# A fused MLP kernel on one core: the transpose of tile 2 moved ahead of weight slab 2 on SyncE's queue

## The chip, the core and the metric

The kernel runs on one core of a Trainium2 chip. The metric is the device time of one execution in microseconds (us), as the median over runs. Beside the timed runs one execution is profiled; its trace has the start and duration of every instruction on each engine, the semaphore events, and the DMA packets. In the profile's rows PE is TensorE's matmul, PEld its weight load, DVE VectorE, ACT ScalarE, POOL GpSimd and SP SyncE. A "q" behind an engine (SPq) marks what its sequencer does, here the issue of a DMA.

## What is computed

A two-layer perceptron with SiLU between the layers, in bfloat16, with x of 2048 x 640, w1 of 640 x 1728 and w2 of 1728 x 640:

```python
def reference(x, w1, w2):
    h = jnp.einsum("bsd,df->bsf", x, w1)
    h = _silu(h)
    out = jnp.einsum("bsf,fd->bsd", h, w2)
    return out
```

## The kernel before

**Layout.** The first layer is computed transposed: `hT` holds h with its 1728 features on partitions (13 tiles of 128 and one of 64) and the 2048 tokens along the free side. A matmul takes 64 columns of `w1s` as weights and streams 512 tokens of `xT`; `step` (line 179) issues the two halves of one feature tile, and the five `k` tiles of the depth 640 accumulate in PSUM. `xT` is x transposed: [128, 5 tiles of depth, 2048 tokens]. x comes from memory through DMA transposes straight into `xT`, w1 through plain loads into `w1s`.

**The opening.** The tokens go in four chunks of 512. For chunk 0 the data have not all arrived when TensorE could begin, so the loop is turned inside out: eight feature tiles (`NO` = 8) hold the eight PSUM banks, and `sweep` runs once for each depth tile k over all eight. Sweep k needs tile k of `xT` and *slab* k of w1 (rows of depth tile k, columns 0 to 1023, 256 KB). Slab 0 comes in two parts: columns 0 to 639 on ScalarE's queue (slab 0a, 160 KB) and 640 to 1023 on SyncE's (slab 0b, 96 KB). Before the first data TensorE runs matmuls on a tile of zeros (`first_dummies`). `opening` then runs sweeps 0, 1 and 2; the lines behind it run 3 and 4. After sweep 4 of a feature tile ScalarE applies SiLU and writes `hT`. Then come feature tiles 8 to 12 of chunk 0, with the remaining columns of w1 (`ld_rest`, `ld_rest2`), and chunks 1 to 3, whose transposes are 15 further DMAs (line 159).

**The queue.** Nearly all DMAs are issued by SyncE, which takes its instructions in order. `early` puts an instruction into the program's first block, ahead of that engine's part in the barrier that closes the block; several calls for SyncE stand there in the order in which they were made. The order of the opening on SyncE is: transpose of tiles 0 and 1; slab 0b; slab 1; slab 2; transpose of tile 2; slab 3; transpose of tiles 3 and 4; slab 4; then, behind the barrier, the rest of w1, the 15 transposes, and w2. `turned` (line 90) issues a transpose, `load` (line 85), called by `slab`, a plain load. Each has a semaphore of its own.

**Who waits.** TensorE alone waits for these transfers. Sweep 0 waits for the transpose of tiles 0 and 1 and slab 0a, and at feature tile 5 (`NA`) for slab 0b; sweeps 1 and 2 wait for their slab and their tile, through

```python
            for k in (1, 2):
                sweep(k, 0, SCH, ld_w1[k], ld_t[k])
```

where `ld_t[1]` is the same event as `ld_t[0]`; sweep 3 waits for slab 3 and the transpose of tiles 3 and 4, sweep 4 for slab 4.

**The second layer** begins when all of h is there. It runs in quads of output tiles whose two halves of the contraction share the array, evicts PSUM by VectorE and ScalarE in turn and stores the output. None of it touches the lines of the change.

Of the kernel before, what the change touches and what calls it, by code (L numbers as in the profile page):

```python
# [9 lines left out]
def bass_standalone__dense_activation_silu__prompt_kernel(  # L10
# [16 lines left out]
    DT = D // P  # L27
    FT = F // P
    FL = F - FT * P
    SCH = 512  # L30
# [10 lines left out]
    with ExitStack() as es:  # L41
# [18 lines left out]
        def sem(name):  # L60
            s = es.enter_context(nc.semaphore(name))
            count[s.name if hasattr(s, "name") else name] = 0
            return [s, 0]

        def tick(ins, s, n=1):
            ins.then_inc(s[0], n)
            s[1] += n
            return (s, s[1])
# [16 lines left out]
        def load(eng, out_ap, in_ap):  # L85
            s = sem(f"s_ld{n_dma[0]}")
            n_dma[0] += 1
            return tick(eng.dma_start(out=out_ap, in_=in_ap), s, 16)

        def turned(c0, c1, k0, k1):  # L90
            s = sem(f"s_tr{n_dma[0]}")
            n_dma[0] += 1
            return tick(sp.dma_start_transpose(
                out=xT[:, k0:k1, c0:c1], in_=xf[c0:c1, k0 * P:k1 * P]), s, 16)

        ET = mybir.EngineType

        def early(emit, engine, arrived=True):
            n = len(nc.main_func.blocks[0].instructions)
            r = emit()  # L100
            lst = nc.main_func.blocks[0].instructions
            new = lst[n:]
            del lst[n:]
            at = next(
                i for i, ins in enumerate(lst)
                if ins.opcode == ("EventSemaphore" if arrived else "Drain") and ins.engine == engine
            )
            lst[at:at] = new
            return r
# [8 lines left out]
        def slab(eng, k, f0=0, f1=NO):  # L118
            return load(eng, w1s[:, k, f0 * P:f1 * P], w1_v[:, k, f0 * P:f1 * P])

        ld_w1 = {}
        ld_t = {}
# [18 lines left out]

        ld_w1b = early(lambda: slab(sp, 0, NA, NO), ET.SP, False)
        ld_w1[1] = early(lambda: slab(sp, 1), ET.SP, False)
        ld_w1[2] = early(lambda: slab(sp, 2), ET.SP, False)
        ld_t[2] = early(lambda: turned(0, SCH, 2, 3), ET.SP, False)
        ld_w1[3] = early(lambda: slab(sp, 3), ET.SP, False)
        ld_t[3] = ld_t[4] = early(lambda: turned(0, SCH, 3, DT), ET.SP, False)
        ld_w1[4] = early(lambda: slab(sp, 4), ET.SP, False)
        CM = CO + 2 * P
        ld_rest = load(sp, w1s[:, :, CO:CM], w1_v[:, :, CO:CM])  # L150
# [259 lines left out]
```

## Time and profile before

| | |
|---|---|
| Median of 3 runs | 124.75 us (124.65 to 124.89) |
| The profiled execution's own time | 124.91 us |
| Its span, first to last instruction | 123.4 us |
| TensorE matmul busy | 121.1 us |
| TensorE weight load busy | 59.5 us |
| ScalarE busy | 38.8 us |
| VectorE busy | 7.0 us |
| DMA, whole span | 10.42 MB |
| Granted TensorE clock, mean | 1.000 |

Times in the trace count from the span's start, so they are 1.5 us short of the device time as a whole (124.91 - 123.4), which lies around the span. In a row of the timeline the first number is the start, the second the length from the first instruction's start to the last one's end, and "x" the count. The square brackets give the idle time of the engine ahead of the row and what ended it. In the list of DMA issues the last number is the time from the issue to the last of the transfer's semaphore increments. A matmul's recorded end is a model, so a TensorE that reads as busy may still have waited inside; the starts of its weight loads are recorded.

### The profile page before, as it was taken

What the parts mean: (1) busy time and instruction counts of PE and PEld (TensorE: products, weight loads), DVE (VectorE), ACT (ScalarE), POOL (GpSimd) and SP (SyncE); (2) the same over time, 40 slices, a digit from 0 to 9 for tenths busy, and PEclk for the clock granted to TensorE, in tenths of its full rate; (3) what the DMA queues carried; (4) which work ended last, traced back from release to release, by engine and by line L of the source; (5) the groups of instructions that cost most, each with busy time, mean ns of one, the idle gap of its engine ahead of it and who ended that gap; (6) DMA issues with size and microseconds to landing.
All of it is one profiled execution on the core that took longest, in us unless ns stands there. A gap on an engine that the chain in (4) does not pass through costs nothing.

```text
span 123.4 us, 2299 instructions
## 1 busy us (share of the span) xinstructions
PE 121.1 (98%) x1057; PEld 59.5 (48%) x1057; DVE 7.0 (6%) x11; ACT 38.8 (31%) x67; POOL 0.3 (0%) x5
## 2 busy tenths in 40 slices
PE   8999999999999999999999999999999999999993
PEld 5455555555555555555544444444444444444452
DVE  0000000000000000000000022002201300222001
ACT  0041985555555555555530011001101200110110
POOL 0000000000000000000000000000000000000000
PEclk9999999999999999999999999999999999999999
DMA  6999945475992000000000005202200220022112
GB/s 142 234 271 302 157 103 108 94 75 92 288 391 70 0 0 0 8 0 0 0 0 5 0 5 115 56 0 106 106 0 5 106 106 0 5 106 106 53 74 86
DMA packets 19482, 10.42 MB, mean 84 GB/s; under 512 B 13457, under 2 KB 18961, under 8 KB 19473
## 3 DMA queue, kind: packets, MB, share of 16 engines
q1 hardware_dynamic: 19184, 10.05, 32.1%
q10 hardware_dynamic: 288, 0.23, 0.8%
q8 instruction: 8, 0.13, 0.5%
q14 instruction: 2, 0.01, 0.0%
HBM read 4.51 MB, written 2.62 MB: 58 GB/s over the span
## 4 chain that ended last, share of the span: by engine, by line
PE 95%; DMA 3%; ACT 0%; issue 0%
PE ps L171 95%; DMA xT<-in_x_dram 3%; ACT o_sb L254 0%
## 5 line engine op out<-in xcount | busy, mean ns | idle before, releaser
L171 PE MATMUL ps<-xT,w1s 128*64 128x512 bf16 x540 | 59.2, 382 | 0.1
L171 PE MATMUL ps<-w2s,hT 64*128 64x512 bf16 (+3 forms) x377 | 46.2, 369 | 0.0
L171 PEld LDWEIGHTS ps<-xT,w1s 128*64 128x64 bf16 x540 | 30.5, 111 | 28.6 <-issue 0.9
L175 ACT ACTIVATE hT<-ps 128x512 bf16<-128x512 f32 x52 | 30.0, 607 | 22.9 <-PE ps L171 22.9
L171 PEld LDWEIGHTS ps<-w2s,hT 64*128 64x128 bf16 (+1 forms) x377 | 21.0, 95 | 24.1 <-issue 0.2
L254 ACT CAST o_sb<-ps 128x512 bf16<-128x512 f32 (+1 forms) x9 | 5.0, 551 | 41.5 <-PE ps L171 41.5
L171 PE MATMUL ps<-hT,w2s 64*128 64x512 bf16 x104 | 11.7, 376 | 0.0
L171 PEld LDWEIGHTS ps<-hT,w2s 64*128 64x128 bf16 x104 | 5.0, 94 | 6.3 <-issue 0.4
L252 DVE CAST o_sb<-ps 128x512 bf16<-128x512 f32 (+1 forms) x8 | 5.4, 675 | 40.5 <-PE ps L171 40.5
L252 DVE CAST oT<-ps 128x512 bf16<-128x512 f32 x2 | 1.4, 692 | 73.8 <-PE ps L171 73.8
L254 ACT CAST oT<-ps 128x512 bf16<-128x512 f32 x2 | 1.2, 586 | 10.6 <-PE ps L171 10.6
L132 PE MATMUL ps<-z 128*128 128x256 bf16 (+1 forms) x15 | 3.3, 419 | 0.4 <-DVE z L125 0.4
L153 ACT ACT_TABLE_LOAD x1 | 1.3, 1283 | 7.1 <-DVEq L395 7.1
L171 PE MATMUL ps<-w2t,hTt 64*128 64x512 bf16 (+2 forms) x17 | 2.9, 363 | 0.0
L132 PEld LDWEIGHTS ps<-z 128*128 128x128 bf16 (+1 forms) x15 | 1.9, 142 | 1.5 <-issue 0.4
L175 ACT ACTIVATE hTt<-ps 128x512 bf16<-128x512 f32 x2 | 1.2, 597 | 1.0 <-PE ps L171 1.0
L171 PEld LDWEIGHTS ps<-w2t,hTt 64*128 64x128 bf16 x17 | 0.9, 94 | 1.1
L171 PE MATMUL ps<-hTt,w2t 64*128 64x512 bf16 x4 | 0.8, 376 | 0.0
L171 PEld LDWEIGHTS ps<-hTt,w2t 64*128 64x128 bf16 x4 | 0.2, 94 | 0.2
L153 ACT ACTIVATE warm<-warm 128x32 f32<-128x32 f32 x1 | 0.2, 229 | 0.0
L125 DVE MEMSET z<- 128x128 uint32 x1 | 0.2, 165 | 0.2 <-issue 0.2
L140 POOL MEMSET warm<- 128x32 f32 x1 | 0.1, 125 | 6.7 <-POOLq L395 6.7
(4 smaller groups left out, 0.4 us busy)
## 6 DMA issues: line engine op xcount, KB each, us to landing
out_dram<-o_sb SPq DMA_DIRECT2D x15, 160.0 KB, 1.8
w2s<-in_w_dram SPq DMA_DIRECT2D x1, 1120.0 KB, 6.1
w1s<-in_w_dram SPq DMA_DIRECT2D x4, 256.0 KB, 3.9
w2s<-in_w_dram SPq DMA_DIRECT2D x1, 960.0 KB, 8.4
w1s<-in_w_dram SPq DMA_DIRECT2D x1, 560.0 KB, 5.5
w1s<-in_w_dram SPq DMA_DIRECT2D x1, 320.0 KB, 4.3
xT<-in_x_dram SPq DMA_TRANSPOSE x18, 3.9
w1s<-in_w_dram ACTq DMA_DIRECT2D x1, 160.0 KB, 2.7
```

The source lines that it names most:

```text
L125: p_z = early(lambda: tick(dve.memset(z[:, :], 0.0), s_dve), ET.DVE, False)
L132: pe.matmul(ps[c0:c0 + w, 3, 0:HB], lhsT=z[:, 0:w], rhs=z[:, :], start=True, stop=True)
L140: p_warm = tick(pool.memset(warm[:, :], 0.0), s_pool)
L153: act.activation(out=warm[:, :], in_=warm[:, :], func=ACT.Silu)
L171: return pe.matmul(o, lhsT=l, rhs=r, start=start, stop=stop, skip_group_check=shared)
L175: r = tick(act.activation(out=out_ap, in_=in_ap, func=ACT.Silu), s_act)
L252: r = tick(dve.tensor_copy(out=out_ap, in_=in_ap), s_dve)
L254: r = tick(act.copy(out=out_ap, in_=in_ap), s_act)
```

## The change

The transpose of tile 2 is made one place earlier on SyncE's queue, ahead of slab 2 instead of behind it. Slabs 2 and 3 then stand next to each other. In the transpose of tiles 3 and 4 the upper bound `DT` is written as 5, which is its value.

```diff
         ld_w1b = early(lambda: slab(sp, 0, NA, NO), ET.SP, False)
         ld_w1[1] = early(lambda: slab(sp, 1), ET.SP, False)
+        ld_t[2] = early(lambda: turned(0, SCH, 2, 3), ET.SP, False)
         ld_w1[2] = early(lambda: slab(sp, 2), ET.SP, False)
-        ld_t[2] = early(lambda: turned(0, SCH, 2, 3), ET.SP, False)
         ld_w1[3] = early(lambda: slab(sp, 3), ET.SP, False)
-        ld_t[3] = ld_t[4] = early(lambda: turned(0, SCH, 3, DT), ET.SP, False)
+        ld_t[3] = ld_t[4] = early(lambda: turned(0, SCH, 3, 5), ET.SP, False)
         ld_w1[4] = early(lambda: slab(sp, 4), ET.SP, False)
```

The order on SyncE is then: transpose of tiles 0 and 1; slab 0b; slab 1; transpose of tile 2; slab 2; slab 3; transpose of tiles 3 and 4; slab 4. The waits of the sweeps are written as before.

## The prediction

> **What bounds the kernel now.** I read the page first: its span line, its busy rows and its chain of work that ended last.
>
> ```profile
> span 123.4 us, 2299 instructions
> PE 121.1 (98%) x1057; PEld 59.5 (48%) x1057; DVE 7.0 (6%) x11; ACT 38.8 (31%) x67; POOL 0.3 (0%) x5
> PE 95%; DMA 3%; ACT 0%; issue 0%
> ```
>
> The chain in order of time then says where those 3% of DMA lie.
>
> ```profile
> 0.00 3.72 DMA xT<-in_x_dram
> 3.72 0.04 issue
> 3.76 117.77 PE ps L171 x1041
> ```
>
> There is one DMA on the path: the first transpose (tiles 0 and 1), which lands at 3.72. From 3.76 to 121.53 TensorE runs matmul after matmul and the chain never leaves it. So the reordered transfers matter only if one of them now lands too late, or if the first transpose moves. A busy PE row does not prove that nothing waits, because matmul ends are modelled; so I went to the weight loads (PEld) in the timeline of the first 30 us, whose starts are not.
>
> ```profile
> 3.76 0.18 PEld L171 LDWEIGHTS ps<-xT,w1s 128*64 128x64 bf16 x4 [0.36 <-DMA xT<-in_x_dram]
> 4.19 0.18 PEld L171 LDWEIGHTS ps<-xT,w1s 128*64 128x64 bf16 x2 [0.25 <-issue]
> 4.62 0.18 PEld L171 LDWEIGHTS ps<-xT,w1s 128*64 128x64 bf16 x2 [0.25 <-issue]
> 5.05 0.18 PEld L171 LDWEIGHTS ps<-xT,w1s 128*64 128x64 bf16 x2 [0.25 <-issue]
> 5.42 24.50 PEld L171 LDWEIGHTS ps<-xT,w1s 128*64 128x64 bf16 x228 [0.19 <-issue]
> ```
>
> A step (`step`, two matmuls of 64 columns) has two loads. The rows before 5.42 hold ten loads, the weights of steps 0 to 4, 0.43 us apart. From 5.42 there are 228 loads, 114 steps, in 24.50 us: 0.215 us a step without a break. So step n (n from 5) loads its weights at 5.42 + 0.215 x (n - 5), and each sweep has eight steps. That gives a **due time** to every transfer: slab 0b (step 5) 5.42; slab 1 (step 8) 6.06; slab 2 and tile 2 (step 16) 7.79; slab 3 and tiles 3, 4 (step 24) 9.51; slab 4 (step 32) 11.23. One load takes 0.11 us (its row in the groups) and its matmul comes a step later, so I estimate that a load may slip by 0.215 - 0.11, about 0.1 us, before a matmul is late.
>
> **Arrivals now.** SyncE's queue in the timeline gives the issues:
>
> ```profile
> 0.00 1.33 SPq L93 DMA_TRANSPOSE xT<-in_x_dram  x1
> 1.38 1.58 SPq L88 DMA_DIRECT2D w1s<-in_w_dram  x3
> 3.01 1.15 SPq L93 DMA_TRANSPOSE xT<-in_x_dram  x1
> 4.20 0.58 SPq L88 DMA_DIRECT2D w1s<-in_w_dram  x1
> 4.82 1.24 SPq L93 DMA_TRANSPOSE xT<-in_x_dram  x1
> 6.10 1.95 SPq L88 DMA_DIRECT2D w1s<-in_w_dram  x3
> ```
>
> Within the row of three at 1.38, narrow windows give slab 0b 1.38 for 0.56, slab 1 2.00 for 0.49, slab 2 2.53 for 0.43. The list of DMA issues, asked one issue at a time, gives the time to landing; two of its answers, slab 2 and tile 2:
>
> ```profile
> w1s<-in_w_dram SPq DMA_DIRECT2D x1, 256.0 KB, 4.0
> xT<-in_x_dram SPq DMA_TRANSPOSE x1, 4.1
> ```
>
> The others are 3.8 (slab 0b), 3.8 (slab 1), 3.7 (slab 3), 4.1 (tiles 3, 4) and 4.4 (slab 4). Issue plus that: slab 0b 5.2, slab 1 5.8, slab 2 6.5, tile 2 7.1, slab 3 7.9, tiles 3 and 4 8.9, slab 4 10.5. Against the due times the margins are 0.2, 0.26, 1.3, 0.7, 1.6, 0.6 and 0.7 us. Nothing is late today; the tight ones are the two **ahead** of the move.
>
> **The change, step by step.** Nothing is added or removed: the same transfers and waits, and `DT` is 5, so the edited transpose of tiles 3 and 4 is the same. Costs:
>
> 1. SP issue. Tile 2 is issued at 2.53 instead of 3.01 and takes 1.15 to 1.24, so until about 3.7; slab 2 follows at 3.72 to 3.77 instead of 2.53, for 0.43 to 0.58; slab 3 comes at 4.2 to 4.4 (was 4.20), tiles 3 and 4 at 4.8 to 5.0 (was 4.82). Slab 2 is the only transfer that is issued later, by 1.2 us. All behind it are off by 0.2 us at most, inside margins of 0.6 and more. SP itself is waited for by no one here.
>
> 2. Arrivals. The landings of now follow each other by what each transfer takes of a full queue: slab 1 to slab 2 0.7, slab 2 to tile 2 0.6, tile 2 to slab 3 0.8, slab 3 to tiles 3 and 4 1.0. With the two swapped: slab 1 5.8, tile 2 6.4, slab 2 7.1, slab 3 7.9, the rest as before. Slab 2 is due at 7.79, so 0.7 us of margin; tile 2 has 1.4. In short, the last of the pair still lands at 7.1. The other bound for slab 2 takes the time from issue to landing as fixed: 3.72 + 3.7 = 7.4 at best and 3.77 + 4.4 = 8.2 at worst, up to 0.4 late. I take 7.1, because the slab rows read 3.7 to 4.0 behind a full queue while slab 0a, with only the first transpose ahead, reads 2.7: most of the difference is queue.
>
> The Trainium skill (Advanced Engine Details and Errata, X-Bar Transpose (TRN2)) says that transposes by DMA are as fast as ordinary ones. The trace disagrees for tile 2: its 128 KB took 0.6 where a slab of 256 KB took 0.7 to 0.8. By the rule tile 2 would take 0.35 and slab 2 would land at 6.85, which would only make its being late less likely.
>
> 3. What lies ahead. A transpose now follows slab 1 directly and its issue starts 0.48 earlier, while the first transpose (lands 3.72), slab 0b and slab 1 are still under way. The trace doesn't show this order. From below: nothing, as these transfers were issued earlier; a gain is excluded for the slabs, which nobody waits for. From above: slab 1 takes the longest time to landing of any slab here, 4.4, and lands at 2.00 + 4.4 = 6.4, 0.34 late, of which 0.1 may be covered. Slab 0b at 1.38 + 4.4 = 5.8 would be 0.36 late; a delay of the one moves the due time of the other, so these don't add up. If the first transpose lost the whole 0.48, half would show, since steps at 0.43 are replaced by steps at 0.215: 0.24. I take nothing, nearer to how the slabs behind the first transpose fare today (3.8 and 3.8, like all others).
>
> Sum: 0 us on the path. The profiled execution has a span of 123.4 and 1.5 around it, 124.91 in all, a little over the median of 124.75; the forecast is **124.75**.
>
> **Rivals.**
>
> *Slab 1 late (slower).* Place: the first load of sweep 1, due at 6.06. Price: slab 1 landing at x costs x - 6.06, less up to 0.1; it decides from a landing of about 6.15, and at 6.4 it costs 0.24 to 0.34: 125.0 to 125.1. For it: the margin of 0.26 is the second smallest of all, and the DMA row is poor just after the first transpose, 49 GB/s in this window of 0.2 us, against 420 at 4.8 to 5.0.
>
> ```profile
> 3.40:3.60 0.20, 0.20 (x2) 0.00 (x0) 0.00 (x0) 0.00 (x0) 0.00 (x0) 1.00 0.53 49
> 4.80:5.00 0.20, 0.20 (x4) 0.00 (x0) 0.00 (x0) 0.00 (x0) 0.00 (x0) 1.00 1.08 420
> ```
>
> (Columns: window, length, busy time and count of PE, PEld, DVE, ACT, POOL, clock, DMA share, GB/s.) So a transpose does something to its neighbours. Against it: slab 2 and slab 3, which have a transpose behind them today, read 4.0 and 3.7; 4.0 would put slab 1 at 6.0, just in time.
>
> *Slab 2 late (slower).* The bound of step 2: up to 8.2, 0.3 to 0.4 late, 124.75 to 125.15. Against it: the queue reading of the 2.7.
>
> *The clock comes at another time (faster or slower).* The loads go from 0.43 to 0.215 us a step between 5.05 and 5.42. Four steps ran slow, 4 x 0.21 = 0.85 us that an earlier turn could save at most: down to 123.9; each step more costs 0.21. Against it: the granted clock reads 1.00 everywhere, and nothing before 5.05 on TensorE is touched; the three runs differ by 0.24, about one such step. The Trainium skill (TensorE: Matmul & The Clock Gate, What's actually happening) holds that the clock is released after a busy window of some 3.4 us that runs free of the kernel's start; by it the turn may move between runs, whatever the queue does, and an idle stretch from a late transfer could push it back. One profile can't show that.
>
> *The order does nothing.* Tile 2 might land at 7.1 all the same. The time is the forecast's.
>
> Faster by any other road is nearly closed: the warm-up matmuls fill PE until about 3.7, so an earlier first transpose is worth under 0.1.
>
> **Chances.** No cost 0.54; slab 1 (or 0b, or the first transpose) late 0.26; slab 2 late 0.10; another clock turn 0.10 (0.08 of it faster). The three runs span 0.2%, so 0.2% (0.25 us) is what counts as no change. Of the first slower case I put 0.22 over that bound, of the second 0.06, of the clock 0.02: slower 0.30. Faster 0.08. Within 0.62. The forecast's own range is 124.5 to 125.0; low 124.45 is the fastest run less one slow step, high 125.3 is the worst of the slabs (125.15) plus the spread of the runs upward (0.14).
>
> **What would show it.** Tile 2's issue at 2.53 landing near 6.4; slab 2's issue at 3.7 landing near 7.1; the long row of weight loads again from about 5.42 with no second row in the first 30 us; the chain again with PE from 3.76 for 117.8. Wrong would be: a gap in the weight loads near 6.06 (slab 1) or 7.79 (slab 2), a first load later than 3.76, or another count of slow steps.

## The result, and the profile after

| | before | changed |
|---|---|---|
| Median, first timing | 124.70 us (4 runs) | 125.38 us (4 runs) |
| Ratio, 95% interval | | 1.0054 (1.0031 to 1.0077) |
| Median, second timing on one chip | 124.71 us (33 runs) | 125.38 us (10 runs) |
| Ratio, 95% interval | | 1.0036 (1.0011 to 1.0062) |
| Span of the profiled execution | 123.4 us | 123.9 us |

The changed kernel is slower by 0.4 to 0.5%; the quotient of the second timing's medians, 1.0054, lies inside its interval. The chain of work of the changed kernel, in order of time (start, length, what):

```profile
0.39 3.31 PE ps L132 x15
3.70 0.02 issue
3.72 118.26 PE ps L171 x1041
```

The chain shows no DMA at all. TensorE starts at 3.72, 0.04 earlier than before, and seems never to stop, yet its stretch is 118.26 instead of 117.77. The weight loads in the timeline say where the 0.5 went:

```profile
3.72 0.19 PEld L171 LDWEIGHTS ps<-xT,w1s 128*64 128x64 bf16 x4 [0.31 <-DMA xT<-in_x_dram]
4.15 0.18 PEld L171 LDWEIGHTS ps<-xT,w1s 128*64 128x64 bf16 x2 [0.24 <-issue]
4.58 0.18 PEld L171 LDWEIGHTS ps<-xT,w1s 128*64 128x64 bf16 x2 [0.24 <-issue]
5.00 0.18 PEld L171 LDWEIGHTS ps<-xT,w1s 128*64 128x64 bf16 x2 [0.24 <-issue]
5.43 0.18 PEld L171 LDWEIGHTS ps<-xT,w1s 128*64 128x64 bf16 x2 [0.24 <-issue]
5.86 0.18 PEld L171 LDWEIGHTS ps<-xT,w1s 128*64 128x64 bf16 x2 [0.24 <-issue]
6.28 23.66 PEld L171 LDWEIGHTS ps<-xT,w1s 128*64 128x64 bf16 x220 [0.24 <-issue]
```

Six steps ran at 0.43 us where four did before; from 6.28 on it is 110 steps in 23.66, 0.215 each, without a break. Two slow steps more, each 0.215 longer than a fast one, make 0.43, and that would explain this profile by the clock alone. It is a trap, as the runs below show. The other view to read is SyncE's queue and the landings (list of DMA issues, one issue at a time: slab 2, slab 3, tiles 3 and 4):

```profile
2.46 1.16 SPq L93 DMA_TRANSPOSE xT<-in_x_dram  x1
3.66 1.05 SPq L88 DMA_DIRECT2D w1s<-in_w_dram  x2
4.76 1.24 SPq L93 DMA_TRANSPOSE xT<-in_x_dram  x1
...
w1s<-in_w_dram SPq DMA_DIRECT2D x1, 256.0 KB, 4.5
w1s<-in_w_dram SPq DMA_DIRECT2D x1, 256.0 KB, 4.5
xT<-in_x_dram SPq DMA_TRANSPOSE x1, 5.1
```

Slab 2 lands at 3.66 + 4.45 = 8.11 (6.55 before), slab 3 at 8.80 (7.90), tiles 3 and 4 at 9.82 (8.96). Sweep 2's first load in this execution is at 8.25 and sweep 3's at 9.97: six slow steps have delayed TensorE just enough for both transfers to be in time. With four, sweep 2 would have been due at 7.79 and would have stood waiting.

The DMA engines moved less in the same stretches. Windows of before, and then of the changed kernel (the last number is GB/s, the one ahead of it the DMA share):

```profile
4.80:5.40 0.60, 0.60 (x6) 0.18 (x2) 0.00 (x0) 0.00 (x0) 0.00 (x0) 1.00 1.04 381
5.40:6.40 1.00, 1.00 (x12) 0.56 (x10) 0.00 (x0) 0.00 (x0) 0.00 (x0) 1.00 1.20 206
8.20:9.00 0.80, 0.80 (x10) 0.45 (x8) 0.00 (x0) 0.40 (x2) 0.00 (x0) 1.00 1.04 266
```

```profile
4.80:5.40 0.60, 0.60 (x4) 0.18 (x2) 0.00 (x0) 0.00 (x0) 0.00 (x0) 1.00 1.29 194
5.40:6.40 1.00, 1.00 (x8) 0.49 (x6) 0.00 (x0) 0.00 (x0) 0.00 (x0) 1.00 0.71 137
8.20:9.00 0.80, 0.80 (x10) 0.44 (x8) 0.00 (x0) 0.34 (x2) 0.00 (x0) 1.00 0.74 146
```

0.6 x (381 - 194) + 1.0 x (206 - 137) + 0.8 x (266 - 146) is 280 KB less in these three; the other windows from 2.60 to 9.00 all but cancel. At the 324 GB/s that the changed kernel moved from 4.00 to 4.80, 280 KB are an estimated 0.86 us, which fits the 0.86 by which tiles 3 and 4 are late.

### The profile page after: what moved, and what is told of

It reads as the page before. It is cut to its first block, busy times and chain, and to the rows that moved or that the text cites. A ratio compares the mean times of both kernels' runs of the same rounds, so it can differ in the third digit from the quotient of the medians.

```text
span 123.9 us, 2299 instructions
## 1 busy us (share of the span) xinstructions
PE 121.6 (98%) x1057; PEld 59.7 (48%) x1057; DVE 6.9 (6%) x11; ACT 38.8 (31%) x67; POOL 0.3 (0%) x5
## 4 chain that ended last, share of the span: by engine, by line
PE 98%; ACT 0%; issue 0%; DVEq 0%
PE ps L171 95%; PE ps L132 3%; ACT o_sb L254 0%; DVEq L395 0%
```

## The experiments

Ratios are to the kernel before on the same chip, with 95% intervals. Landings are those of the last of 16 DMA engines, from the increments of each transfer's semaphore in the trace.

**1. Both kernels again.** No edit.

> The kernel before once more, for a second look at its slow steps. Theory S (slab 2 lands at about 8.1 us with the new order and holds sweep 2 back): the number of slow steps (loads 0.43 us apart) is a matter of chance, so it may differ from the four seen; each step more makes this execution 0.21 longer and nothing else changes. Theory C (the order of the queue moves the moment at which TensorE goes from 0.43 to 0.215 us a step): four slow steps again, turn at about 5.4. Both: ratio 1.000.

> The changed kernel once more. Theory S: slab 2 lands at 8.0 to 8.2 again, so the first load of sweep 2 is at 8.05 to 8.25 (before: 7.79) whatever the number of slow steps is; if only four steps are slow, a gap of about 0.3 us stands in the weight loads ahead of sweep 2. Theory C: six slow steps again and no gap ahead of sweep 2. Both: ratio 1.004 to 1.006.

Measured: the kernel before 0.9985 (0.9963 to 1.0006), 124.21 to 125.14 in 12 runs; the changed kernel 1.0036 (1.0011 to 1.0062), six slow steps again, slab 2 at 8.18, sweep 2's first load at 8.25 and no gap. The second profile of before is another picture than the first (timeline, weight loads):

```profile
3.54 0.79 PEld L171 LDWEIGHTS ps<-xT,w1s 128*64 128x64 bf16 x10
5.01 0.36 PEld L171 LDWEIGHTS ps<-xT,w1s 128*64 128x64 bf16 x6 [0.69 <-DMA w1s<-in_w_dram]
5.66 12.02 PEld L171 LDWEIGHTS ps<-xT,w1s 128*64 128x64 bf16 x114 [0.29 <-DMA w1s<-in_w_dram]
```

No step is slow here: the first five have their weights within 0.79. TensorE then waits for slab 0b (landed 4.97) and for slab 1 (landed 5.62). So the number of slow steps changes from execution to execution of one kernel, and when TensorE is fast from the start the slabs bound it, in the old order as well: sweep 1 can't begin before 5.66 in this execution. That six came twice with the changed kernel was not yet told from an effect of the change.

**2. Sweep 2 without slab 2**, on the changed kernel and, as a control, on the one before. `kw` is the slab whose weights a step takes.

```diff
-            for k in (1, 2):
-                sweep(k, 0, SCH, ld_w1[k], ld_t[k])
+            sweep(1, 0, SCH, ld_w1[1], ld_t[1])
+            wait(pe, ld_t[2])
+            for ft in range(NO):
+                step(ft, 2, ft, 0, SCH, kw=1)
...
-            sweep(k, 0, SCH, ld_w1[k], ld_t[k])
+            sweep(k, 0, SCH, ld_w1[2], ld_w1[k], ld_t[k])
```

> The changed kernel, but sweep 2 takes slab 1's weights in place of slab 2's, so that it waits for tile 2 alone; slab 2 is loaded as before and waited for by sweep 3 (the output isn't the reference's). Theory S: the cost is gone, ratio 0.998 to 1.001. Theory C: six slow steps and the cost stays, ratio 1.004 to 1.006. If both hold, in between.

> The same edit on the kernel before: sweep 2 takes slab 1's weights and slab 2 is waited for by sweep 3 (the output isn't the reference's). Control. Both theories: ratio 0.999 to 1.001, since slab 2 lands 1.3 us ahead of its use there.

Measured: the control 0.9998 (0.9975 to 1.0021). The changed kernel 1.0040 (1.0020 to 1.0060): the cost stays, as Theory C had it. But the profile shows another reason than C's:

```profile
3.56 0.19 PEld L171 LDWEIGHTS ps<-xT,w1s 128*64 128x64 bf16 x4 [0.16 <-DMA xT<-in_x_dram]
3.99 4.72 PEld L171 LDWEIGHTS ps<-xT,w1s 128*64 128x64 bf16 x44 [0.24 <-issue]
9.87 20.21 PEld L171 LDWEIGHTS ps<-xT,w1s 128*64 128x64 bf16 x189 [1.16 <-issue]
```

One slow step, then 44 loads without a break, and then TensorE stands for 1.16 us ahead of sweep 3, whose first load is at 9.87: tiles 3 and 4 landed at 9.77. The row names "issue", not the DMA, but the chain of work in order of time names the transpose:

```profile
4.76 5.01 DMA xT<-in_x_dram
9.77 0.14 issue
9.90 100.45 PE ps L171 x928
```

So a second transfer is late too, and it took over. Theory F came out of this.

**3. Sweep 3 without tiles 3 and 4 as well.**

```diff
-        for k in range(3, DT - 1):
-            sweep(k, 0, SCH, ld_w1[2], ld_w1[k], ld_t[k])
-        wait(pe, ld_w1[4], ld_t[4])
+        for ft in range(NO):
+            step(ft, 2, ft, 0, SCH, kw=1)
+        wait(pe, ld_w1[2], ld_w1[3], ld_w1[4], ld_t[4])
```

> The changed kernel; sweep 2 takes slab 1's weights and sweep 3 tile 2 with slab 1's weights, so that neither slab 2 nor tiles 3 and 4 are waited for before sweep 4 (the output isn't the reference's). Theory F (with the new order slab 2 at 8.1 and tiles 3 and 4 at 9.8 are each a floor of the same height, so taking away one alone gained nothing): now the cost is gone, ratio 0.998 to 1.001. Theory C (the order moves the turn of the clock): the cost stays, ratio 1.003 to 1.006.

Measured: 1.0009 (0.9989 to 1.0029), so no cost is left that the runs can tell. Its weight loads:

```profile
3.80 0.79 PEld L171 LDWEIGHTS ps<-xT,w1s 128*64 128x64 bf16 x10 [0.45 <-DMA xT<-in_x_dram]
4.96 0.36 PEld L171 LDWEIGHTS ps<-xT,w1s 128*64 128x64 bf16 x6 [0.36 <-DMA w1s<-in_w_dram]
5.67 24.31 PEld L171 LDWEIGHTS ps<-xT,w1s 128*64 128x64 bf16 x228 [0.36 <-DMA w1s<-in_w_dram]
```

The queue's order is the changed one, the slow steps are absent, and sweep 1 begins at 5.67 as in the second profile of before.

So the changed order does not by itself bring six slow steps: in the nine profiles whose first four issues on SyncE are the changed order's, their number goes from none to six. And what the change costs is that sweeps 2 and 3 can't begin before slab 2 and before tiles 3 and 4; the interval without these waits still leaves room for 0.3%, so that all of it lies there is likely and not shown. (The edit drops the wait for slab 3 too, which lands 1.0 ahead of tiles 3 and 4.) The same edit was not tried on the kernel before. In the control's profile tiles 3 and 4 land at 8.93 and sweep 3's first load, at 9.03, comes 0.23 after the load of the step ahead of it, so there was little to gain.

Sized: sweep 3 at 9.87 in experiment 2 means a sweep 1 at 9.87 - 16 x 0.215 = 6.43, against 5.67 here: 0.76 for executions with few slow steps (the two spans are 123.6 and 122.9), 0.68 by the medians. In the first profile of the changed kernel the two transfers ask for the same: 8.11 - 8 x 0.215 and 9.82 - 16 x 0.215 both mean a sweep 1 at 6.4.

**4. Why slab 2 lands at 8.1.** First, tiles 3 and 4 behind slab 4 as well:

```diff
         ld_w1[3] = early(lambda: slab(sp, 3), ET.SP, False)
-        ld_t[3] = ld_t[4] = early(lambda: turned(0, SCH, 3, 5), ET.SP, False)
         ld_w1[4] = early(lambda: slab(sp, 4), ET.SP, False)
+        ld_t[3] = ld_t[4] = early(lambda: turned(0, SCH, 3, 5), ET.SP, False)
```

> The changed order, with the transpose of tiles 3 and 4 put behind slab 4 as well. Slab 2 is issued at 3.7 as in the changed kernel. Theory W (plain loads crawl while a transpose is being issued and prepared, here that of tiles 3 and 4 at 4.8): slab 2 lands at 6.9 to 7.3 and slab 3 below 8.0. Theory J (plain loads crawl just behind a transpose in the queue): slab 2 again at 8.0 to 8.2. Theory Q (a fixed time of 4.0 to 4.5 from issue to landing): slab 2 at 7.7 to 8.2. The time itself: tiles 3 and 4 are issued at 5.4 and should land at 9 to 9.9, so ratio 0.999 to 1.006.

Measured: slab 2 at 8.51, slab 3 at 9.10, tiles 3 and 4 at 10.85; ratio 1.0114 (1.0087 to 1.0142). Slab 2 is later than any of the three theories had it, and tiles 3 and 4 and the time are outside what was expected. W's values for slab 2 held for the middle engine (7.02), but not for the last. Here both late transfers are seen to hold TensorE up in the weight loads, slab 2 ahead of sweep 2 and tiles 3 and 4 ahead of sweep 3:

```profile
8.55 1.44 PEld L171 LDWEIGHTS ps<-xT,w1s 128*64 128x64 bf16 x16 [1.23 <-DMA w1s<-in_w_dram]
10.96 19.13 PEld L171 LDWEIGHTS ps<-xT,w1s 128*64 128x64 bf16 x179 [0.97 <-issue]
```

Then SyncE was made to wait, on the changed order: before the transpose of tiles 3 and 4 until slab 2 had landed ("held", the second added line), before slab 2 until tile 2 had landed ("gap", the first), or both. Only the landings of these single runs are read; their times were 126.44 and 127.21 (held), 125.90 (gap) and 127.26 (both).

```diff
         ld_t[2] = early(lambda: turned(0, SCH, 2, 3), ET.SP, False)
+        early(lambda: wait(sp, ld_t[2]), ET.SP, False)
         ld_w1[2] = early(lambda: slab(sp, 2), ET.SP, False)
         ld_w1[3] = early(lambda: slab(sp, 3), ET.SP, False)
+        early(lambda: wait(sp, ld_w1[2]), ET.SP, False)
         ld_t[3] = ld_t[4] = early(lambda: turned(0, SCH, 3, 5), ET.SP, False)
```

> The changed order, but SyncE waits for slab 2 to have landed before it issues the transpose of tiles 3 and 4. Read by the landing of slab 2 (issued at 3.7), not by the time, which must be some 2 us longer, as tiles 3 and 4 come at 10.5 to 11.5. Theory W (the issue and preparation of a transpose on the same queue holds up some DMA engine's plain packets): slab 2 at 6.8 to 7.3 and the 16 engines within 0.4 of each other. Theory J (plain packets just behind a transpose straggle, whatever is issued): slab 2 at 7.9 to 8.5 as in the changed kernel.

> The kernel that holds tiles 3 and 4 back until slab 2 has landed, once more. Read by the landing of slab 2, taken from that of the first transpose: 3.9 in the run before this one, 4.2 to 4.6 in the four profiles of the changed order. Theory W: 3.6 to 4.0 again. Theory J: 4.2 or more.

> The changed order, but SyncE waits for tile 2 to have landed (near 6.0) before it issues slab 2, slab 3 and, at once behind them, tiles 3 and 4: plain loads with no transpose ahead of them in the engines, but with one being issued beside them. Read by the time of slab 2 from issue to landing, last engine. Theory W: it straggles, 3.4 to 4.2, last engine 0.7 or more behind the median. Theory J: 2.7 to 3.1, engines within 0.4. The time itself is 2 us longer or more.

> As x_gap, and tiles 3 and 4 are held until slab 2 has landed: neither a transpose ahead nor one beside. Both theories: slab 2 from issue to landing 2.6 to 3.1, engines within 0.4 of each other. If it straggles all the same, the cause is neither.

| | tile 2 landed | slab 2 issued | slab 2 landed: first, 9th, last engine |
|---|---|---|---|
| before | 7.13 | 2.53 | 5.55, 6.49, 6.55 |
| changed, profile 1 | 6.04 | 3.66 | 6.63, 7.21, 8.11 |
| changed, profile 2 | 6.08 | 3.71 | 6.67, 6.78, 8.18 |
| sweep 2 without slab 2 | 5.86 | 3.65 | 6.48, 6.99, 8.08 |
| sweeps 2 and 3 without | 6.14 | 3.67 | 6.74, 7.32, 7.98 |
| held | 5.62 | 3.67 | 6.28, 6.64, 7.30 |
| held, again | 5.80 | 3.67 | 6.40, 6.53, 7.47 |
| gap | 5.60 | 5.62 | 7.64, 7.93, 8.19 |
| gap and held | 5.62 | 5.64 | 7.68, 7.98, 8.15 |

With a gap slab 2 takes 2.5 to 2.6 us from issue to landing and the engines finish within 0.6, the last one 0.2 to 0.3 behind the ninth, whether or not a transpose is issued beside it: W falls as a cause of its own. So does Q: from issue to landing slab 2 took 4.3 to 4.5 in the changed order, 3.6 and 3.8 held, and 2.6 and 2.5 with a gap. Directly behind the transpose it lands 1.8 to 2.2 after tile 2, the last engine 0.7 to 1.4 behind the ninth; held, still 1.7 after it and 0.7 to 0.9.

So most of the lateness goes with standing directly behind tile 2 while tile 2 is under way, as J has it, and tiles 3 and 4 on the same queue add some 0.4 to that. J is not shown by this: one held kernel landed at the upper edge of W's range and the other between the two theories, and a gap leaves nothing else under way on the queue either, not only no transpose. The last one to four of the 16 engines are late, by more than 0.3 behind the ninth: by the ninth, slab 2 lands at 6.8 to 7.3 in the changed order.

**5. Slabs 0b and 1 behind the first transpose.**

```diff
         ld_w1[1] = early(lambda: slab(sp, 1), ET.SP, False)
-        ld_t[2] = early(lambda: turned(0, SCH, 2, 3), ET.SP, False)
         ld_w1[2] = early(lambda: slab(sp, 2), ET.SP, False)
         ld_w1[3] = early(lambda: slab(sp, 3), ET.SP, False)
+        early(lambda: wait(sp, ld_w1[1]), ET.SP, False)
+        ld_t[2] = early(lambda: turned(0, SCH, 2, 3), ET.SP, False)
```

> Slab 0b, 1, 2 and 3 first, then SyncE waits for slab 1 to have landed before it issues the transpose of tile 2 and the rest. Read by the landings of slab 0b and slab 1, which have the first transpose ahead of them and no transpose issued beside them. Theory W: slab 0b below 4.5, slab 1 below 5.1. Theory J: slab 0b 4.9 to 5.6, slab 1 5.6 to 6.2. The time is longer by about 1 us in either case (tile 2 near 8.5).

Measured: slab 0b at 4.49, slab 1 at 5.36, single run 126.59. Slab 0b just meets W's bound of 4.5, and slab 1 lies between the two theories. The first transpose landed at 3.41 here, and from there slab 1 took 1.95, against 2.09 in the first profile of before and 1.85 in that of the changed kernel. A small gain at most.

**6. Why slab 3 does not suffer in the old order.** There it stands directly behind tile 2, and yet it lands 0.8 to 1.0 after it (7.13 to 7.90 in the first profile, 6.89 to 7.77 in the second).

```diff
         ld_t[2] = early(lambda: turned(0, SCH, 2, 3), ET.SP, False)
+        early(lambda: wait(sp, ld_w1b), ET.SP, False)
         ld_w1[3] = early(lambda: slab(sp, 3), ET.SP, False)
```

> The order of before, but SyncE waits for slab 0b to have landed (5.0 to 5.2) before it issues slab 3, so that slab 3 is issued some 0.9 later. In the old order slab 3 lands only 0.8 to 1.0 after tile 2, while in the new order slab 2 lands 1.8 to 2.2 after tile 2 (1.7 with tiles 3 and 4 held). Theory P (a plain load is held up behind a transpose if it is issued less than some 2 us before that transpose is through, as slab 2 is in the new order; slab 3 in the old order is issued 2.3 to 2.9 us before tile 2 lands): now slab 3 is issued 1.7 to 2.0 us before tile 2 lands, and lands 1.5 or more after it. Theory N (the lead doesn't matter, it is the place in the queue): 0.8 to 1.1 after it.

> The same kernel once more, as one profile has shown a spread of 0.3 in such landings. Theory P: slab 3 lands 1.5 or more after tile 2. Theory N: 0.8 to 1.1.

Measured: slab 3 issued 1.87 and 1.88 before tile 2 landed, and landing 1.01 and 0.99 after it. Theory P falls. In all these profiles of the old order slab 3's last engine is within 0.1 of the ninth, so J is no rule either: why the same neighbour costs 1.0 there and 2.1 in the new order stays open, and with it the cause of the late engines.

**7. Other orders.** On the changed kernel, tile 2 behind slab 3; on the kernel before, one transpose of tiles 2 to 4 in place of tile 2's; and, on the changed kernel, slabs 2 to 4 on ScalarE's queue after the first transpose has landed.

```diff
-        ld_t[2] = early(lambda: turned(0, SCH, 2, 3), ET.SP, False)
         ld_w1[2] = early(lambda: slab(sp, 2), ET.SP, False)
         ld_w1[3] = early(lambda: slab(sp, 3), ET.SP, False)
+        ld_t[2] = early(lambda: turned(0, SCH, 2, 3), ET.SP, False)
```

> The other way: the transpose of tile 2 goes behind slab 3 (slab 0b, 1, 2, 3, tile 2, tiles 3 and 4, slab 4). Theory W: no transpose is issued between 1.3 and 3.6, so slab 0b and slab 1 come sooner, below 4.6 and 5.2. Theory J: slab 0b 5.0, slab 1 5.6 as before, since both stand behind the first transpose still. Tile 2 (issue 3.6) should land at 7.2 to 7.7, tiles 3 and 4 at 8.8 to 9.2. Time: ratio 0.997 to 1.003, faster if slab 1's lead is worth something.

Measured: 1.0026 (1.0006 to 1.0046). Slab 0b at 5.57 and slab 1 at 6.23, later than before and than either theory; one engine alone was late, as 15 had slab 0b through at 4.26. Tile 2 landed at 8.15, outside what was expected.

```diff
         ld_w1[2] = early(lambda: slab(sp, 2), ET.SP, False)
-        ld_t[2] = early(lambda: turned(0, SCH, 2, 3), ET.SP, False)
+        ld_t[2] = ld_t[3] = ld_t[4] = early(lambda: turned(0, SCH, 2, 5), ET.SP, False)
         ld_w1[3] = early(lambda: slab(sp, 3), ET.SP, False)
-        ld_t[3] = ld_t[4] = early(lambda: turned(0, SCH, 3, DT), ET.SP, False)
```

> The order of before, but the transposes of tile 2 and of tiles 3 and 4 made as one DMA at the place of tile 2 (slab 0b, 1, 2, tiles 2 to 4, slab 3, slab 4). One issue of some 1.3 us falls away. Theory W: slab 3 and 4 are no longer slowed and land below 8.3 and 9.3; the three tiles land at 7.9 to 8.4, which is late for sweep 2 (due 7.4 to 7.8), ratio 1.001 to 1.004. Theory Q: slab 3 at 4.35 + 4 = 8.3, tiles at 3.0 + 4.1 to 5 = 7.1 to 8.0, ratio 0.998 to 1.002.

Measured: 1.0028 (1.0009 to 1.0046). The one issue took 2.31 us, about as much as the two that it replaces (1.15 and 1.24), so that none fell away; the tiles landed at 8.14, slab 3 at 8.76 and slab 4 at 9.45, the two slabs later than W had them.

```diff
-        ld_w1[2] = early(lambda: slab(sp, 2), ET.SP, False)
-        ld_w1[3] = early(lambda: slab(sp, 3), ET.SP, False)
         ld_t[3] = ld_t[4] = early(lambda: turned(0, SCH, 3, 5), ET.SP, False)
-        ld_w1[4] = early(lambda: slab(sp, 4), ET.SP, False)
+        early(lambda: wait(act, ld_t[0]), ET.Activation, False)
+        ld_w1[2] = early(lambda: slab(act, 2), ET.Activation, False)
+        ld_w1[3] = early(lambda: slab(act, 3), ET.Activation, False)
+        ld_w1[4] = early(lambda: slab(act, 4), ET.Activation, False)
```

> A try at a better version: slabs 2, 3 and 4 on ScalarE's queue (issued there once the first transpose has landed), SyncE issues slab 0b, slab 1, tile 2 and tiles 3, 4 one after the other. Tile 2 lands at 6.0 to 6.3, tiles 3 and 4 at 7.2 to 8.0 by either theory; slab 2 (issue near 3.8) at 6.8 to 7.5 if the two queues share the engines evenly, slab 3 near 8.2, slab 4 near 9: then every floor is below the kernel before's, ratio 0.996 to 1.000. If the plain packets are held up by the issue of tiles 3 and 4 on the other queue as well (Theory W at its strongest), slab 2 at 8 and ratio 1.003 to 1.006.

Measured: 1.0107 (1.0068 to 1.0145). Slab 2 at 8.42; tile 2 had 15 engines through at 6.63 and the last at 8.12; tiles 3 and 4 at 10.45, all later than either expectation. A second queue did not take the plain loads out of the transposes' way.

The kernel of experiment 6 had given 124.34 and 124.36 in its single runs, so it was timed:

> The order of before with slab 3 held until slab 0b has landed, timed: two single runs gave 124.34 and 124.36 beside 125.0 of the kernel before. If that was chance (the kernel before alone spreads from 124.2 to 125.4 with the moment at which TensorE turns to 0.215 us a step): ratio 0.999 to 1.001. If slabs 0b and 1 gain by the quieter queue (they landed at 5.0 and 5.6, and 4.8 and 5.4): ratio 0.996 to 0.999.

Measured: 1.0014 (0.9994 to 1.0035), so the two single runs show no gain. Its chain of work:

```profile
1.39 3.82 DMA w1s<-in_w_dram
5.21 0.04 issue
5.25 115.92 PE ps L172 x1031
```

Slab 0b, landed at 5.21, is the transfer on it: again the floor of the old order. No order that was timed beats the kernel before.

## Why the prediction was wrong

- **Start of TensorE, first transpose, slabs 0b and 1** (step 3: no cost): right. The first transpose landed at 3.68, slab 0b at 4.79, slab 1 at 5.53, all earlier than before; the rival "slab 1 late" did not come.
- **Issues on SyncE** (step 1): the times were right to 0.1: 2.46, 3.66, 4.28, 4.76. "All behind it are off by 0.2 us at most" was right of the issues and wrong of the landings.
- **Arrivals** (step 2): this is the step that failed. It took 7.1 for slab 2, by swapping the distances between landings; it was 8.11, almost the other bound of the same step (8.2, the time from issue to landing taken as fixed). The distance between two landings did not go along with the transfer: behind tile 2 the last engine was 0.7 to 1.4 us behind the ninth, where in the old order, behind slab 1, it had been 0.06. The choice between the bounds leaned on slab 0a, a load with no transpose directly ahead on its own queue. Why the last engines are late stays open.
- **What stands behind slab 2**: not priced. Tiles 3 and 4 land about 1.0 after the last engine of slab 3: 7.90 and 8.96 before; 8.80 and 9.82 after. The trace's packet records show what held them in the changed kernel: half of the transpose's 1024 packets ran before 8.6, but 20 of them, begun between 7.29 and 8.32, all ended between 8.62 and 8.66, soon after the last slab packet (8.45), and only then came the other half. The first profile of before has no such held packet. So the late engines made tiles 3 and 4 late by 0.86, and taking slab 2 out alone gained nothing (experiment 2). Their margin of 0.6 was that of an execution with four slow steps; with none, the second profile of before, they land at 8.78 and are used at 8.93.
- **The price of "slab 2 late"**: the rival that came true was put at 0.3 to 0.4 at most, and the median moved by 0.68. Its due time, 7.79, came from an execution with four slow steps. With none, sweep 1 starts at 5.66 and a wait costs time from 5.66 + 8 x 0.215 = 7.38 on; 8.11 is 0.73 late. The same single profile gave step 3's remark that a gain is excluded for slabs that nobody waits for: in the second profile TensorE waits for slabs 0b and 1.
- **The clock at another time**: the turn moves from execution to execution, none to four slow steps in the old order's profiles and none to six in the changed order's. In both profiles of the changed kernel it hid the wait.
- **What would show it**: a gap at 7.79 in the weight loads was named as the sign of a late slab 2. In neither profile of the changed kernel is there one, and the cost was there; the slow steps had filled it. The other sign, another count of slow steps, came, and pointed at the clock.

## What to carry to other kernels

Work out a transfer's margin for the fastest way in which its consumer can run, not for the one execution that was profiled, and look for the next transfer that becomes the floor before pricing the first. On a queue that mixes DMA transposes and plain loads, read the landing of the last engine, not of the typical one: in every profile here a transpose landed only after the last engine of the load ahead of it on its queue, so one straggler can move everything behind it. When two late transfers have the same height, removing either alone shows nothing; remove both before dropping the theory.

## What the hardware showed that was not expected

The moment at which TensorE goes from 0.43 to 0.215 us a step is not fixed: four slow steps and none in two profiles of the kernel before, six in both of the changed one, none in the changed one of experiment 3. In the 33 runs the kernel before spread from 124.37 to 125.35. The granted clock read 1.00 in all of them, so the profile's clock column does not show it; the spacing of the weight loads does. That the turn is the clock's is borne out by the clock records in the trace files, which eight of the 19 profiles have: each of them begins where that profile's loads turn to 0.215 us a step, at 5.35 in the first profile of before (between the loads at 5.05 and 5.42), and at 3.49 to 5.83 over all eight. The Trainium skill (TensorE: Matmul & The Clock Gate, What's actually happening) says that the clock is released by a busy window of about 3.4 us that runs free of the kernel's start; the changing count, none to six, agrees with it. So does the length of those clock records, 119.47 us in five of them and 122.88 in three: 35 and 36 times 3.413.

In the opening, the issue of a DMA transpose took SyncE 1.15 to 1.33 us for one tile or two, and 2.31 for three (experiment 7), against 0.33 to 0.58 for a slab.
